# Two heads with rows in another order on the partitions, three stores in fifteen parts

## The chip, the cores and the metric

One core of a Trainium2 chip runs the program. The metric is device time in microseconds (us) of one execution. TensorE (PE), VectorE (DVE), ScalarE (ACT), GpSimd (POOL) and SyncE (SP) each run their own list of instructions in order; they wait for each other and for transfers on semaphores. Transfers (DMAs) are issued here by SP, ACT and POOL, and 16 DMA engines carry them out.

## The reference, cut to what matters

A decoder block for one token and all its gradients: attention with 32 heads over a cache of 8192 keys and values, and a gated MLP beside it. The outputs are the block's output and the gradients of its inputs, the caches among them.

```python
xn = _layernorm(x)
q  = (xn @ wq).reshape(1, 1, 32, 128).transpose(0, 2, 1, 3)
p  = softmax(einsum("bhqd,bhkd->bhqk", q, k_cache) * 128 ** -0.5)
o  = einsum("bhqk,bhkd->bhqd", p, v_cache)
out = x + o.transpose(0, 2, 1, 3).reshape(1, 1, 4096) @ wo + (silu(xn @ w1) * (xn @ w3)) @ w2
# returned: out, and the vjp of grad_out: d x, d k_cache, d v_cache, d wq, d wo, d w1, d w3, d w2
```

Each head reads 2 MB of K and 2 MB of V (bf16) and writes 2 MB of dK and 2 MB of dV, which are outer products: a row of dV is a probability times the head's output gradient, a row of dK a score gradient times q. No sum over the keys depends on their order.

## The kernel before

A head's K, V, dK and dV are tiles of 128 partitions with 64 rows of 128 elements each: partition p holds rows 64p to 64p + 63 of the head, 16 KB in one piece of device memory (`kc`, `vc`, `dkc`, `dvc`). The work runs over the heads in one loop, written out by hand; the program keeps the order in which each engine's instructions are written. While head h is finished, head h + 1 has its scores computed:

- `product` (L365, L367): DVE multiplies K or V with the broadcast vector into T, PE sums it over the elements.
- `row_max`, `exps`, `probs`, `row_dots`, `dscores`: softmax and its gradient, as [128, 64] tiles.
- `outer` (L380, L387, L394): the tile `ot` of dV, then that of dK. ACT makes 16 of its 64 columns, DVE the others, in two halves. After the second half POOL issues one store of 2 MB (L394). The last two heads are stored in halves by SP instead (L392).
- `load_v(h + 2)` and `load_k(h + 3)`, both on SP (L117, L110), each behind an `outer`.

Buffers set what may be in flight: three tiles for K, two for V, four for `ot` (`kpool`, `vpool`, `opool`). A load waits until the tile it overwrites has been read, an `outer` until the store of the `ot` four before it has landed.

Weights go beside that. `wq` is kept for eight heads at once (`wq_all`, 5 columns `ci` of 1024 elements on each partition) and overwritten with its gradient. When a group of eight heads is finished, `finish_steps` stores the gradient: the first column at once (L331), the other four go into the list `columns`. `outer_v` takes up to two from the list behind each following store of `ot` (L396), all on POOL. This falls behind the stores of dV and dK of head 9 for the first eight heads and of head 17 for the second; later groups are stored otherwise (`late`). SP also loads later columns of `wq` in `wq_columns` (L139), and ACT loads and stores `wo`.

Of the kernel before, what the change touches and what calls it, by code (L numbers as in the profile page):

```python
# [16 lines left out]
P = 128  # L17
# [4 lines left out]
def kernel(  # L22
# [22 lines left out]
    nc = tc.nc  # L45
    H = A_k_cache.shape[1]
# [5 lines left out]
    NC = D // P  # L52
    J = SK // P
    JH = J // 2
# [4 lines left out]
    GW = 8  # L59
# [19 lines left out]
    ps_o = ctx.enter_context(tc.tile_pool(name="ps_o", bufs=1, space=PSUM))  # L79
    ps_w = ctx.enter_context(tc.tile_pool(name="ps_w", bufs=3, space=PSUM))  # L80

    kc = A_k_cache.rearrange("b h (p j) d -> (b h) p j d", p=P)
    vc = A_v_cache.rearrange("b h (p j) d -> (b h) p j d", p=P)
    dkc = out_2.rearrange("b h (p j) d -> (b h) p j d", p=P)
    dvc = out_3.rearrange("b h (p j) d -> (b h) p j d", p=P)

    wq_v = A_wq.rearrange("(p ci) n -> p ci n", ci=NC)
    dwq_v = out_4.rearrange("(p ci) n -> p ci n", ci=NC)
# [9 lines left out]
    with tc.manual_schedule(engines=ORDERED):  # L98
# [8 lines left out]
        def load_k(h):  # L107
            pool, tag = ((opool, "o"), (vpool, "V"))[h] if h < 2 else (kpool, "K")
            Kt = pool.tile([P, J, DH], BF16, name="Kt", tag=tag)
            nc.sync.dma_start(Kt[:], kc[h])  # L110
            kv_tiles[h] = kv_tiles.get(h, [None, None])
            kv_tiles[h][0] = Kt

        def load_v(h):
            pool, tag = (opool, "o") if h == 1 else (vpool, "V")
            Vt = pool.tile([P, J, DH], BF16, name="Vt", tag=tag)
            nc.sync.dma_start(Vt[:], vc[h])  # L117
            kv_tiles[h] = kv_tiles.get(h, [None, None])
            kv_tiles[h][1] = Vt

# [3 lines left out]
        def store(dst, src, later=False):  # L124
            if later:
                late.append((dst, src))
            else:
                nc.gpsimd.dma_start(dst, src)
# [176 lines left out]
        def finish_steps(g):  # L305
            G_ = grp[g]
            wo_g = G_["wo"]
            on, on_bf = on_cols(g)
            behind_o.append((g, on_bf))
            yield  # L310
            assert not behind_o
            for r in range(GH):
                nc.scalar.activation(wo_g[:, r, :], g_bc_bf[:], ACTF.Copy, scale=on[:, r:r + 1])
                if r == 1:
                    yield
            if g == NG - 2:
                store(dwo_v[g], wo_g[:], True)
            else:
                nc.scalar.dma_start(dwo_v[g], wo_g[:])
            yield  # L320
            b, k = divmod(g, HB)
            for ci in range(NC):
                nc.scalar.activation(G_["wq"][:, ci, :], G_["dqbc"][:].rearrange("p h d -> p (h d)"),
                                     ACTF.Copy, scale=xn_col[:, ci:ci + 1])
            if g < NG - HB and k == HB - 1:
                cols = slice(b * GW * DH, (b + 1) * GW * DH)
                if g == NG - HB - 1:
                    store(dwq_v[:, :, cols], G_["wq_all"][:], True)
                else:
                    columns.extend((dwq_v[:, ci, cols], G_["wq_all"][:, ci, :]) for ci in range(NC))  # L330
                    nc.gpsimd.dma_start(*columns.pop(0))  # L331
            if g >= NG - HB:
                store(dwq_v[:, :, g * GH * DH:(g + 1) * GH * DH], G_["wq"], True)
            grp.pop(g)
# [35 lines left out]
        def outer(st, vec, w2, wf, dst, h, half):  # L370
            outer_v(st, vec, w2, dst, h, half, outer_s(st, vec, wf, half))

        def outer_s(st, vec, wf, half):
            if half == 0:
                st.ot = opool.tile([P, J, DH // 2, 2], BF16, name="ot", tag="o")
            j1 = (half + 1) * JH
            if wf is None:
                return j1
            for j in range(ACT_J):
                nc.scalar.activation(st.ot[:, j1 - ACT_J + j].rearrange("p a b -> p (a b)"), vec, ACTF.Copy,  # L380
                                     scale=wf[:, half, j:j + 1])
            return j1 - ACT_J

        def outer_v(st, vec, w2, dst, h, half, j1):
            j0 = half * JH
            n = j1 - j0
            nc.vector.tensor_tensor(st.ot[:, j0:j1],  # L387
                                    vec.rearrange("p (a b) -> p a b", b=2).unsqueeze(1).to_broadcast([P, n, DH // 2, 2]),
                                    w2[:, j0:j1, :].unsqueeze(2).to_broadcast([P, n, DH // 2, 2]), ALU.mult)
            rows = st.ot[:].rearrange("p j a b -> p j (a b)")  # L390
            if h >= H - TAIL:
                nc.sync.dma_start(dst[h][:, j0:j0 + JH, :], rows[:, j0:j0 + JH, :])  # L392
            elif half:
                nc.gpsimd.dma_start(dst[h], rows)  # L394
                for _ in range(2 if len(columns) > 2 else len(columns)):
                    nc.gpsimd.dma_start(*columns.pop(0))  # L396

        columns = []

        def row_max(st):  # L400
# [193 lines left out]
        for b in range(NB):  # L594
            rows, src = (P, w2t[:, b, :]) if b < NF else (REST, w2r)
# [37 lines left out]
        def gap():  # L633
            if steps and next(steps[0], "end") == "end":
                steps.pop(0)
# [13 lines left out]
        def wq_columns(h, part):  # L649
            b, r = divmod(h, GW)  # L650
            if 0 < b < H // GW - 1 and (r, part) in WQ_AT:
                load_wq(b + 1, *WQ_AT[r, part])

        for h in range(H - 1):
            n = new_head(h + 1) if h + 1 < H else None
            c = hs.pop(h)
            g, hh = divmod(h, GH)
            if n:
                product(n, "S", 0)
            probs(c)  # L660
            outer(c, c.do, c.P2, c.Pf, dvc, h, 0)
            if prev:
                keep_dq(prev)
            gap()
            row_dots(c)
            attend(c)
            turn_wq(c)
            if n:
                product(n, "S", 1)
            outer(c, c.do, c.P2, c.Pf, dvc, h, 1)  # L670
            if h + 2 < H:
                load_v(h + 2)
            wq_columns(h, 0)
            if hh == 1 and 0 < g < NG - 1:
                load_wo(g + 1, nc.scalar)
            gap()
            dscores(c)
            outer(c, c.q, c.U2, c.Uf, dkc, h, 0)
            keep_wq(c)
            if n:  # L680
                row_max(n)
                product(n, "DP", 0)
            outer(c, c.q, c.U2, c.Uf, dkc, h, 1)
            if h == 0:
                load_k(4)
            elif 1 < h < H - 3:
                load_k(h + 3)
            wq_columns(h, 1)
            wq_columns(h, 2)
            if h == H - 3:  # L690
                for dst, src in late:
                    store(dst, src)
            gap()
            if n:
                exps(n)
                product(n, "DP", 1)
            weights(c)
            gap()
            if hh == 1 and g + 1 < NG:
                steps.append(prep_steps(g + 1))  # L700
            if hh == 2:
                gap()
            prev = c

        c = hs.pop(H - 1)
# [1 line left out]
        probs(c)  # L707
        attend(c)
        turn_wq(c)
        outer(c, c.do, c.P2, None, dvc, H - 1, 0)  # L710
        row_dots(c)
        outer(c, c.do, c.P2, c.Pf, dvc, H - 1, 1)
        keep_dq(prev)
        while steps:
            gap()
        keep_wq(c)
        dscores(c)
        outer(c, c.q, c.U2, None, dkc, H - 1, 0)
        weights(c)
        keep_dq(c)  # L720
        on, on_bf = on_cols(g)
        on_sums(g, on_bf)
        outer(c, c.q, c.U2, None, dkc, H - 1, 1)
        dwq_t = tpool.tile([P, NC, GH * DH], BF16, name="dwq_t", tag="T")
        for ci in range(NC):
            nc.scalar.activation(dwq_t[:, ci, :], c.G["dqbc"][:].rearrange("p h d -> p (h d)"),
# [63 lines left out]
```

## Time and profile before

| | |
|---|---|
| time, median of 3 runs | 732.8 us (732.59 to 733.54) |
| time of the profiled execution | 732.82 us |
| its span, first to last instruction | 731.0 us |
| DVE, PE, ACT, POOL busy | 630.7, 558.0, 461.8, 47.4 us |
| bytes moved | 303.70 MB, 415 GB/s over the span |
| queue 1 (SP), queue 0 (POOL), queue 10 (ACT) | 155.41, 139.42, 7.87 MB |

The profile gives busy time for each engine, a row of 40 equal slices of the span for the DMA engines (busy tenths and GB/s), the chain of work that ended last (followed back from the end, each piece to what released it), groups of instructions, waits, and for every kind of DMA the median time from its issue to its landing. The trace behind it also records when each of a DMA's semaphore counts arrived, and start, duration, size and queue of every DMA packet, though not which of the 16 engines carried it.

### The profile page before, as it was taken

The page shows a single profiled execution, that of the slowest core. Times are in us where ns is not written, and L with a number is a line of the kernel's source. Part 1 is how long each engine was busy: PE and PEld are TensorE (multiplying, and loading weights), DVE is VectorE, ACT ScalarE, POOL GpSimd, SP SyncE. Part 2 cuts the span into 40 slices and gives each one's busy share as a digit, 9 for nine tenths or more (in the row PEclk, how much of TensorE's full clock was granted, in tenths as well). Part 3 has the DMA queues.
Part 4 walks back from the last instruction along what each step waited for, and adds up shares of the span by engine and source line. Part 5 has one row for each costly group of instructions (what it writes and reads, how often), then busy time and mean ns, then how long its engine had stood idle before and what let it go on. Part 6 is the DMA issues. An engine that isn't in the chain of part 4 may idle for free.

```text
span 731.0 us, 15785 instructions
## 1 busy us (share of the span) xinstructions
PE 558.0 (76%) x6513; PEld 325.8 (45%) x6513; DVE 630.7 (86%) x720; ACT 461.8 (63%) x1391; POOL 47.4 (6%) x92
## 2 busy tenths in 40 slices
PE   5776888887887797886788787578767888877860
PEld 3654445453544454443444444344444445444440
DVE  4789999999999796997899888689598998999990
ACT  2176666876768476775577756476476866777650
POOL 0010000000000100100000110100000000000100
PEclk9699788787888778778787677677888768877665
DMA  8999999999999999999999999999999999999992
GB/s 357 413 421 427 428 429 429 428 427 429 429 429 428 428 428 427 426 429 427 429 428 429 427 430 426 429 429 423 418 408 400 423 424 428 430 432 429 418 414 110
DMA packets 26790, 303.70 MB, mean 415 GB/s; under 512 B 3084, under 2 KB 3150, under 8 KB 9054
## 3 DMA queue, kind: packets, MB, share of 16 engines
q1 hardware_dynamic: 13778, 155.41, 50.6%
q0 software_dynamic: 11200, 139.42, 45.0%
q10 hardware_dynamic: 1740, 7.87, 2.6%
q8 instruction: 51, 0.84, 0.4%
q14 instruction: 21, 0.17, 0.1%
HBM read 151.34 MB, written 151.34 MB: 414 GB/s over the span
## 4 chain that ended last, share of the span: by engine, by line
DMA 53%; DVE 28%; PE 9%; ACT 5%; issue 2%; SPq 0%; ACTq 0%; DVEq 0%; POOLq 0%
DMA out_dram<-ot 44%; DVE T L365 13%; DVE ot L387 10%; DMA out_dram<-wo_g 4%; ACT ot L380 4%; DMA Vt<-in_A_v_cache_dram 3%; PE psS L367 2%; PE psDP L367 2%; DMA dbc<-in_B_w_dram 2%; DVE S_sb L402 1%; PE ob L429 1%; PE dx_ps L546 1%; PE up_ps L521 1%; DVE DP_sb L436 1%; PE gate_ps L521 1%
## 5 line engine op out<-in xcount | busy, mean ns | idle before, releaser
L367 PE MATMUL psDP<-T,ident_bf 128*128 128x512 bf16 x512 | 183.6, 523 | 59.9 <-DVE T L365 59.8
L367 PEld LDWEIGHTS <-ident_bf 128*128 128x128 bf16 x1024 | 121.6, 121 | 225.2 <-issue 174.5
L380 ACT ACTIVATE ot<-qs_g,Uf 128x128 bf16<-128x128 bf16 x496 | 151.5, 389 | 74.2 <-DMA out_dram<-ot 32.3
L380 ACT ACTIVATE ot<-do_g,Pf 128x128 bf16<-128x128 bf16 x504 | 154.0, 389 | 6.4 <-DMA out_dram<-ot 5.4
L367 PE MATMUL psS<-T,ident_bf 128*128 128x512 bf16 x512 | 149.8, 446 | 9.3 <-DVE T L365 9.2
L365 DVE TENSOR_TENSOR T<-Kt,qs_g 128x4096 bf16<-128x4096 bf16 x64 | 146.5, 2288 | 8.2 <-DMA Kt<-in_A_k_cache_dram 8.1
L365 DVE TENSOR_TENSOR T<-Vt,do_g 128x4096 bf16<-128x4096 bf16 x64 | 146.0, 2282 | 4.5 <-ACT do_g L284 2.5
L387 DVE TENSOR_TENSOR ot<-qs_g,U 128x3072 bf16<-128x3072 bf16 (+1 forms) x64 | 113.2, 1769 | 36.2 <-DMA out_dram<-ot 36.2
L387 DVE TENSOR_TENSOR ot<-do_g,P 128x3072 bf16<-128x3072 bf16 (+1 forms) x64 | 112.8, 1763 | 7.9 <-DMA out_dram<-ot 6.9
L394 POOL DMA_DIRECT2D out_dram<-ot x60 | 32.0, 534 | 573.7 <-DVE Uf L449 292.6
L451 PEld LDWEIGHTS <-Kt 128*128 128x128 bf16 x2048 | 58.1, 98 | 11.9 <-issue 9.8
L451 PE MATMUL ob<-U,Kt 128*128 128x1 bf16 x2048 | 57.3, 164 | 1.6 <-DVE U L444 1.5
L429 PEld LDWEIGHTS <-Vt 128*128 128x128 bf16 x2048 | 56.6, 97 | 0.0
L429 PE MATMUL ob<-P,Vt 128*128 128x1 bf16 x2048 | 56.0, 163 | 0.0
L406 PE MATMUL sm<-ident_f,mrow 128*128 128x128 f32 x64 | 19.2, 390 | 33.5 <-DVE mrow L404 33.5
L470 ACT ACTIVATE dq_diag<-ident_bf,odq 128x128 bf16<-128x128 bf16 x32 | 12.8, 400 | 45.8 <-DVE odq L466 45.8
L423 ACT ACTIVATE Pf<-E,rZ 128x16 f32<-128x16 f32 x32 | 9.8, 305 | 40.8 <-DVE rZ L419 40.7
L258 ACT COPY woT<-ps_t 128x512 bf16<-128x512 bf16 x40 | 23.0, 577 | 15.3 <-PE ps_t L253 15.3
L406 PEld LDWEIGHTS sm<-ident_f,mrow 128*128 128x128 f32 x64 | 12.0, 234 | 35.5 <-DVE mrow L404 33.8
L440 PE MATMUL sm<-rdot,ones_fc 128*128 128x1 f32 x64 | 11.3, 245 | 20.8 <-DVE junk L439 20.8
L440 PEld LDWEIGHTS sm<-rdot,ones_fc 128*128 128x128 f32 x64 | 10.6, 192 | 33.5 <-DVE junk L439 31.1
L402 DVE TENSOR_REDUCE S_sb<-psS 128x64 f32<-128x512 f32 x32 | 21.9, 684 | 3.2 <-PE psS L367 3.1
(160 smaller groups left out, 510.4 us busy)
## 6 DMA issues: line engine op xcount, KB each, us to landing
out_dram<-ot POOLq DMA_DIRECT2D x60, 2048.0 KB, 31.2
Kt<-in_A_k_cache_dram SPq DMA_DIRECT2D x32, 2048.0 KB, 25.9
Vt<-in_A_v_cache_dram SPq DMA_DIRECT2D x32, 2048.0 KB, 19.2
out_dram<-ot SPq DMA_DIRECT2D x8, 1024.0 KB, 16.4
out_dram<-wo_g ACTq DMA_DIRECT2D x6, 640.0 KB, 15.5
wo_g<-in_A_wo_dram ACTq DMA_DIRECT2D x6, 640.0 KB, 15.6
wq<-in_A_wq_dram SPq DMA_DIRECT2D x2, 1280.0 KB, 20.6
out_dram<-wq POOLq DMA_DIRECT2D x10, 256.0 KB, 39.8
```

Of the source, the lines that this page charges most:

```text
L258: nc.scalar.copy(woT[:], ps_t[:])
L365: nc.vector.tensor_tensor(T[:], src[:, :, ds_], vec[:, ds_].unsqueeze(1).to_broadcast([P, J, DHH]), ALU.mult)
L367: nc.tensor.matmul(ps[:], lhsT=ident_bf[:], rhs=T[:, :, RUN * i:RUN * (i + 1)], start=(half == 0 and i == 0), stop=(half == 1 and i == DHH ...
L380: nc.scalar.activation(st.ot[:, j1 - ACT_J + j].rearrange("p a b -> p (a b)"), vec, ACTF.Copy, scale=wf[:, half, j:j + 1])
L387: nc.vector.tensor_tensor(st.ot[:, j0:j1], vec.rearrange("p (a b) -> p a b", b=2).unsqueeze(1).to_broadcast([P, n, DH // 2, 2]), w2[:, j0: ...
L394: nc.gpsimd.dma_start(dst[h], rows)
L402: nc.vector.tensor_reduce(st.S[:], st.ps["S"][:], AX.X, ALU.add)
L406: nc.tensor.matmul(st.sm[:, 8:8 + P], lhsT=mrow[:].to_broadcast([P, P]), rhs=ident_f[:], start=True, stop=True, skip_group_check=True)
L429: nc.tensor.matmul(st.ob[:, 0:1], lhsT=st.V[:, j, :], rhs=st.P2[:, j, 0:1], start=(j == 0), stop=(j == J - 1), skip_group_check=True)
L440: nc.tensor.matmul(st.sm[:, 4:5], lhsT=ones_f, rhs=rdot[:], start=True, stop=True, skip_group_check=True)
L451: nc.tensor.matmul(st.ob[:, 1:2], lhsT=st.K[:, j, :], rhs=st.U2[:, j, 0:1], start=(j == 0), stop=(j == J - 1), skip_group_check=True)
L521: nc.tensor.matmul(ps[0:rows, b:b + 1], lhsT=block(wt[:, ci, :], b), rhs=xn_col_bf[:, ci:ci + 1], start=(ci == 0), stop=(ci == NC - 1))
```

## The change

For heads 9 and 17, K, V, dK and dV are placed on the partitions in another order (`rows_of` with `mixed`). A head's 128 pieces of 16 KB are numbered 0 to 127; before, partition p holds piece p. Now there are 16 lanes of 8 partitions: partition 8a + n holds piece 16n + a. Loads and stores of these heads use the same order, so each piece returns to its place.

Three of their tiles (dK of head 9, dV and dK of head 17) are no longer stored by one DMA of 128 partitions. POOL stores lanes 0 to 14, 120 partitions, and SP stores lane 15, 8 partitions, later (`behind_k`, behind `load_k` in the same head). Around each of the three, two columns of the `wq` gradient that were stored by two DMAs of 128 partitions are stored by three DMAs that each take both columns: 5 partitions ahead of the store, 78 and 45 behind it. The other tile of the two heads, dV of head 9, is still one DMA, followed by two single columns.

```diff
+    LANES = 16
+    MIXED = {9: "K", 17: "VK"}
+    def rows_of(ap, mixed):
+        if not mixed:
+            return ap.rearrange("b h (p j) d -> (b h) p j d", p=P)
+        return ap.rearrange("b h (n a j) d -> (b h) a n j d", a=LANES, j=J)
+    SPAN = P // LANES
...
-            nc.sync.dma_start(Kt[:], kc[h])
+            nc.sync.dma_start(Kt[:], rows_of(A_k_cache, h in MIXED)[h])
...
-            nc.sync.dma_start(Vt[:], vc[h])
+            nc.sync.dma_start(Vt[:], rows_of(A_v_cache, h in MIXED)[h])
...
-                    columns.extend((dwq_v[:, ci, cols], G_["wq_all"][:, ci, :]) for ci in range(NC))
-                    nc.gpsimd.dma_start(*columns.pop(0))
+                    wq_g = G_["wq_all"]
+                    def pair(ci):
+                        return lambda p0, p1: nc.gpsimd.dma_start(dwq_v[p0:p1, ci:ci + 2, cols], wq_g[p0:p1, ci:ci + 2, :])
+                    nc.gpsimd.dma_start(dwq_v[:, 0, cols], wq_g[:, 0, :])
+                    for ci, which in ((1, "V"), (3, "K")):
+                        if which in MIXED[b * GW + GW + 1]:
+                            columns.append(pair(ci))
+                        else:
+                            columns.extend((dwq_v[:, c, cols], wq_g[:, c, :]) for c in (ci, ci + 1))
...
+            out = rows_of({"K": out_2, "V": out_3}[dst], h in MIXED)[h]
             if h >= H - TAIL:
-                nc.sync.dma_start(dst[h][:, j0:j0 + JH, :], rows[:, j0:j0 + JH, :])
+                nc.sync.dma_start(out[:, j0:j0 + JH, :], rows[:, j0:j0 + JH, :])
             elif half:
-                nc.gpsimd.dma_start(dst[h], rows)
-                for _ in range(2 if len(columns) > 2 else len(columns)):
+                n = min(2, len(columns))
+                if dst in MIXED.get(h, ""):
+                    store_past(out, rows, columns.pop(0))
+                    n = 0
+                else:
+                    nc.gpsimd.dma_start(out, rows)
+                for _ in range(n):
                     nc.gpsimd.dma_start(*columns.pop(0))
+        def store_past(out, rows, pairs):
+            n = (LANES - 1) * SPAN
+            pairs(0, 5)
+            nc.gpsimd.dma_start(out[0:LANES - 1], rows[0:n])
+            pairs(5, 83)
+            pairs(83, P)
+            behind_k.append((out[LANES - 1], rows[n:P]))
...
             elif 1 < h < H - 3:
                 load_k(h + 3)
+            while behind_k:
+                nc.sync.dma_start(*behind_k.pop(0))
```

The calls of `outer` pass "K" or "V" in place of `dkc` and `dvc`.

More of the change, by code (lines that the diff above doesn't have):

```diff
@@ L80 @@
     ps_w = ctx.enter_context(tc.tile_pool(name="ps_w", bufs=3, space=PSUM))
[L82 to L85, printed above, removed]
+    LANES = 16
[5 more added lines that the diff above has]
+    SPAN = P // LANES
     wq_v = A_wq.rearrange("(p ci) n -> p ci n", ci=NC)
@@ L390, in outer_v @@
             rows = st.ot[:].rearrange("p j a b -> p j (a b)")
+            out = rows_of({"K": out_2, "V": out_3}[dst], h in MIXED)[h]
             if h >= H - TAIL:
-                nc.sync.dma_start(dst[h][:, j0:j0 + JH, :], rows[:, j0:j0 + JH, :])
+                nc.sync.dma_start(out[:, j0:j0 + JH, :], rows[:, j0:j0 + JH, :])
             elif half:
-                nc.gpsimd.dma_start(dst[h], rows)
-                for _ in range(2 if len(columns) > 2 else len(columns)):
-                    nc.gpsimd.dma_start(*columns.pop(0))
+                n = min(2, len(columns))
[5 more added lines that the diff above has]
+                for _ in range(n):
+                    nc.gpsimd.dma_start(*columns.pop(0))
+        def store_past(out, rows, pairs):
[5 more added lines that the diff above has]
+            behind_k.append((out[LANES - 1], rows[n:P]))
+        behind_k = []
         columns = []
@@ L660 @@
             probs(c)
-            outer(c, c.do, c.P2, c.Pf, dvc, h, 0)
+            outer(c, c.do, c.P2, c.Pf, "V", h, 0)
             if prev:
@@ L669 @@
                 product(n, "S", 1)
-            outer(c, c.do, c.P2, c.Pf, dvc, h, 1)
+            outer(c, c.do, c.P2, c.Pf, "V", h, 1)
             if h + 2 < H:
@@ L677 @@
             dscores(c)
-            outer(c, c.q, c.U2, c.Uf, dkc, h, 0)
+            outer(c, c.q, c.U2, c.Uf, "K", h, 0)
             keep_wq(c)
@@ L682 @@
                 product(n, "DP", 0)
-            outer(c, c.q, c.U2, c.Uf, dkc, h, 1)
+            outer(c, c.q, c.U2, c.Uf, "K", h, 1)
             if h == 0:
@@ L709 @@
         turn_wq(c)
-        outer(c, c.do, c.P2, None, dvc, H - 1, 0)
+        outer(c, c.do, c.P2, None, "V", H - 1, 0)
         row_dots(c)
-        outer(c, c.do, c.P2, c.Pf, dvc, H - 1, 1)
+        outer(c, c.do, c.P2, c.Pf, "V", H - 1, 1)
         keep_dq(prev)
@@ L717 @@
         dscores(c)
-        outer(c, c.q, c.U2, None, dkc, H - 1, 0)
+        outer(c, c.q, c.U2, None, "K", H - 1, 0)
         weights(c)
@@ L722 @@
         on_sums(g, on_bf)
-        outer(c, c.q, c.U2, None, dkc, H - 1, 1)
+        outer(c, c.q, c.U2, None, "K", H - 1, 1)
         dwq_t = tpool.tile([P, NC, GH * DH], BF16, name="dwq_t", tag="T")
```

## The prediction

> **What bounds the kernel now.** I read the page first: slices of the span, queues, chain.
>
> ```profile
> DMA  8999999999999999999999999999999999999992
> GB/s 357 413 421 427 428 429 429 428 427 429 429 429 428 428 428 427 426 429 427 429 428 429 427 430 426 429 429 423 418 408 400 423 424 428 430 432 429 418 414 110
> ...
> DMA 53%; DVE 28%; PE 9%; ACT 5%; issue 2%; SPq 0%; ACTq 0%; DVEq 0%; POOLq 0%
> DMA out_dram<-ot 44%; DVE T L365 13%; DVE ot L387 10%; DMA out_dram<-wo_g 4%; ACT ot L380 4%; DMA Vt<-in_A_v_cache_dram 3%; PE psS L367 2%; PE psDP L367 2%; DMA dbc<-in_B_w_dram 2%; DVE S_sb L402 1%; PE ob L429 1%; PE dx_ps L546 1%; PE up_ps L521 1%; DVE DP_sb L436 1%; PE gate_ps L521 1%
> ...
> out_dram<-ot POOLq DMA_DIRECT2D x60, 2048.0 KB, 31.2
> Kt<-in_A_k_cache_dram SPq DMA_DIRECT2D x32, 2048.0 KB, 25.9
> Vt<-in_A_v_cache_dram SPq DMA_DIRECT2D x32, 2048.0 KB, 19.2
> ```
>
> The 16 DMA engines are the bound: 428 GB/s in nearly every slice, and the chain waits 44% of the span for stores of `ot`. So only bytes, idle engines or an uneven share can change the time; the change moves no byte less. Two places are below 428: slices 28 to 33 and the end. Next, therefore, the DMA view of the last 31 us (a slice of its GB/s row is 0.775 us), and the same view of an early and a late stretch.
>
> ```profile
> GB/s 455 396 423 312 439 386 428 391 449 402 402 428 423 412 428 381 419 385 414 360 366 343 117 48 21 26 26 26 26 32 21 32 21 26 32 24 26 13 0 0
> ```
> ```profile
> out_dram<-ot POOLq DMA_DIRECT2D x9, 2048.0 KB, 18.0
> Vt<-in_A_v_cache_dram SPq DMA_DIRECT2D x5, 2048.0 KB, 15.0
> ```
> ```profile
> out_dram<-ot POOLq DMA_DIRECT2D x10, 2048.0 KB, 32.4
> Vt<-in_A_v_cache_dram SPq DMA_DIRECT2D x5, 2048.0 KB, 17.3
> ```
>
> From 718.6 to 729 us the rate is 26 GB/s, a sixteenth of 428: one engine works alone. The second and third fences are 60:150 and 560:660: a store of 2 MB took 18.0 us to land, later 32.4, while loads stayed at 15 to 17. The trace's semaphore record tells why. Every transfer of `ot` counts 16 arrivals, one an engine. For the store issued at 144.2 the 15th came at 161.8 and the 16th at 163.0; at 326.4: 358.3 and 363.0; at 638.4: 655.9 and 671.5. One engine falls behind, by 1, 5, then 15 us, where it stays because the other fifteen wait for the buffers that it still holds. The chain shows that hold:
>
> ```profile
> 599.04 32.33 DMA out_dram<-ot
> ...
> 638.42 33.10 DMA out_dram<-ot
> 671.54 1.76 DVE ot L387
> ...
> 713.41 0.19 DVEq L785
> ```
>
> In the packet record each packet starts 3 to 4 ns before its predecessor on the engine ends, so packets can be strung together. Undisturbed engines take 611 ns for 16 KB (26.9 GB/s). Stretches of the late one have none of the 51 instruction fetches and yet run slower: 154.95 to 202.11 us at 26.05 GB/s, which is 629 ns a packet. Strung back from the end, its last packet ends at 729.26; the others end between 716.9 and 718.5.
>
> **The change, part by part.** Sums are made on the profiled execution: last packet 729.26, span 731.0 (1.8 after it), time 732.82 (1.8 more), which is the median 732.8 to 0.02.
>
> (1) *The store without one lane.* 7680 packets for 60 stores are 128 a store, 8 an engine. Storing 15 lanes of 8 partitions takes 8 packets from one engine, three times: 24 packets. If that is the late engine, 24 x 0.629 = 15.1 us leave it. If it is another, the late one keeps all.
>
> (2) *The left lanes*, issued by SP: 8 partitions of 16 KB, three times. If they go to eight engines, one packet each, those get 3 x 0.61 = 1.8 us more, 1.9 on the late one if it is among them.
>
> (3) *The pairs.* The same 512 KB of `wq_all` in parts of 20, 312 and 180 KB in place of two DMAs of 256 KB. An even dealing of whole partitions needs a divisor: 5, 13 (of 78) and 15 (of 45) engines, my assumption. Then an engine gets between 16 and 40 KB where it had 32: at most 8 KB more, three times, 0.9 us; at least 1.8 less.
>
> (4) *Issue.* One more POOL DMA a tile, 0.54 us, the store itself 0.54 later, behind the part of five. POOL is 6% busy and its stores are behind 18 to 32 us of landing, so nothing. But POOL also waits for semaphores that are still in use:
>
> ```profile
> 426.27 0.54 POOL L396 DMA_DIRECT2D out_dram<-wq  x1 [3.04 <-DMA out_dram<-ot]
> 431.69 0.33 SPq L117 DMA_DIRECT2D Vt<-in_A_v_cache_dram  x1
> 436.63 0.33 SPq L110 DMA_DIRECT2D Kt<-in_A_k_cache_dram  x1
> 437.30 0.54 POOL L394 DMA_DIRECT2D out_dram<-ot  x1 [10.49 <-DMA out_dram<-ot]
> ```
> POOL's DMAs go round eight semaphores, and each waits until the eighth before it has landed. Two more in head 17 make the store of K17 (422.16) wait for that of V16 (landed 426.0) and that of K18 (443.78) for V17's (450.3; its 15th arrival 444.3): 1 to 6.5 us later, behind a ring filled for 20 us. Taken as 0, with 6.5 as the upper end.
>
> (5) *SP.* The left lanes stand behind `load_k` and wait for the finished `ot`: in head 9 from 244.08 to 249.64, in head 17 from 415.71 to 422.16. Behind them stands only `load_v`, at 263.92 and 431.69, so 9 us or more hide it. V17's lane is issued some 10 us after its store and lands in some 15, inside the store's own 38. Zero; uncovered, some 6 us once.
>
> (6) *Rows in another order.* Loads and stores of heads 9 and 17 remain packets of 16 KB. No row shows this order. Bounds: 0, or doubled packets (rival C). I take 0: the nearest row, 64 rows of 1280 B on half the partitions, took 55 ns a packet, in line with 84 ns for 2048 B. Less than 0 is excluded, as 611 ns is the fastest seen.
>
> (7) *Which engine.* The last DMA of ACT has five rows of 256 B, and one of these packets (717.235) is in the late engine's string. Their five closing packets came at 715.713, 715.788, 715.863, then 716.554 and 718.038, the last on the late engine. Dealt in order, 75 ns apart, the late one is fourth or fifth. If POOL deals parts in rotation from the first engine, five parts take the first five, the 15 parts run from the sixth round to the fourth, and the fifth is left out. 5 + 13 + 15 + 15 = 48 then ends where it began. I find both numberings plausible, neither shown; hence the miss below.
>
> Sum for the late engine: 15.1 - 1.9 - 0.9 = 12.3 us less, 729.3 - 12.3 = 717.0. The others end at 718.5, get up to 1.8 + 0.5 more, and win back what they idled for it: slices 28 to 33 lack 78 GB/s against 429, 78/429 x 18.3 = 3.3 us. 718.5 + 2.3 - 3.3 = 717.5, which ends last. Can the computing follow? The wait up to 671.54 could end at 655.9; next the DVE needs V31, which landed at 685.2 and was first used at 692.9, so its chain can move 7.7 us earlier; 3.3 are needed. Last packet 717.5, so 717.5 + 1.8 + 1.8 = **721.1 us**. Ends: perfect sharing, mean end of the others 717.4 + 10.8/16 - 3.3 = 714.8, and slices 38 and 39 filled too (26 GB/s short, 1.1 us), 713.7, time 717.3; no idle won back, 720.8, time 724.4.
>
> What the skill says of part 7: the Trainium skill, DMA: Bandwidth & Descriptors, section "Latency and other measured facts", has engines 7 and 15 usually slower. By that the skip would miss, which part 7's packets speak against. The dealing assumed in parts 3 and 7 (the largest count up to 16 that divides, in rotation on POOL's queue, the lowest engines on ACT's) is stated in its section "Why a DMA increments its semaphore by 16 and not by 1"; no run here shows it.
>
> The Trainium skill, SBUF — State Buffer, section "Door 1: The DMA port swizzle", puts partitions 32 apart on the same port. By it lanes of eight neighbouring partitions could meet at a port, which speaks for rival C; the 55 ns row does not show it.
>
> **Rivals.**
>
> B: *the skip misses.* The late engine keeps its 15.1 us and gets parts 2 and 3: between 1.9 - 1.8 = 0.1 and 1.9 + 0.4 = 2.3 us more, 732.9 to 735.1. For it: no row shows POOL's dealing, or that engine numbers of two queues agree. Against it: part 7's fifth place in both counts. 0.13, of which 0.05 for a late engine in eighth or last place (735.1 or 733.3).
>
> C, the slower side: *two engines meet in the new order.* Place: the eight transfers of heads 9 and 17, 64 packets an engine. Price: 64 times what a packet gains over 611 ns; at 800 ns it eats the 12 us, and doubled it costs 39, so 732.8 - 12 + 39 = 760. For it: nothing in the rows; against it the 55 ns, and that half the traffic goes elsewhere at any time. 0.07, decided from 800 ns on.
>
> D: *hit, but some is lost* to POOL's semaphore waits (up to 6.5 us) or packets between 611 and 800 ns: 724.4 to 731. 0.09.
>
> **How the numbers follow.** A hit as summed: 0.71, 717.3 to 724.4, at 721.1. With D that is 0.80 in 717.3 to 731, the range; B and C are left out. A difference of 0.2%, 1.5 us, is what a measurement of this kernel can tell. Faster: 0.71 + 0.09 = 0.80. Same: of B the part below 734.3, 0.07. Slower: the rest of B 0.06 and C 0.07, 0.13.
>
> **What would show it.** Right: the lone 26 GB/s at the end is gone or under 2 us; the 16th arrival of late stores is within 5 us of the 15th; stores at 560:660 land in under 25 us; slices 28 to 33 are at 425 or more; the chain's wait for `ot` is under 30%. Part 1 alone is right if the lag drops by 4 to 5 us after K9 (250) and by 8 to 10 after head 17 (420). Wrong: a lone engine still at work for 10 us at the end (B); packets of heads 9 and 17 over 700 ns, GB/s under 400 near 200 to 290 or 375 to 460 us (C); POOL waits over 10 us after 426 (D). I would also be wrong if computing ended last: then the rate falls off for all engines at once, before the last store is issued.

## The result, and the profile after

The changed kernel takes 743.13 us (median of 4 runs, 741.55 to 745.22); the kernel before, beside it on the same chip, 732.69 us (732.34 to 733.54). The ratio is 1.0142, 95% interval [1.0116, 1.0169]: 10.4 us slower, where 721.1 was predicted. The profiled execution took 741.55 us with a span of 739.1. The ratios below leave out one run as slow, 740.64 us of the run without SP's 8 partitions, because it lies over 1.5% above the fastest of its kernel.

The page of the kernel after: slices (of 18.5 us here), chain, DMA issues.

```profile
DMA  9999999999999999999999999999999999999995
GB/s 356 412 422 426 430 427 427 430 430 423 410 394 427 427 427 401 428 421 429 420 364 412 427 410 398 368 413 423 427 390 395 433 419 430 430 428 430 424 419 233
...
DMA 51%; DVE 31%; PE 9%; ACT 5%; issue 1%; SPq 0%; ACTq 0%; DVEq 0%; POOLq 0%
...
out_dram<-ot POOLq DMA_DIRECT2D x57, 2048.0 KB, 31.2
Kt<-in_A_k_cache_dram SPq DMA_DIRECT2D x32, 2048.0 KB, 23.8
Vt<-in_A_v_cache_dram SPq DMA_DIRECT2D x32, 2048.0 KB, 18.9
...
out_dram<-ot POOLq DMA_DIRECT2D x3, 1920.0 KB, 38.5
```

The three stores of 120 partitions are there, and the bytes are the same (303.70 MB). But the GB/s row, flat at 426 to 430 before from slice 4 to 27, has holes: slice 12 (394), 21 (364), 25 and 26 (398 and 368). The windows view, by 100 us, shows what kind of hole this is. Its last three columns are granted clock, busy share of the DMA engines, GB/s; first the kernel before, then after.

```profile
200.00:300.00 100.00, 78.46 (x876) 43.80 (x873) 86.65 (x94) 65.22 (x199) 9.14 (x17) 0.78 1.01 428
300.00:400.00 100.00, 77.69 (x944) 44.93 (x944) 88.16 (x97) 69.87 (x215) 4.82 (x9) 0.77 1.01 428
400.00:500.00 100.00, 73.51 (x801) 42.02 (x800) 82.29 (x92) 63.50 (x192) 8.64 (x16) 0.73 1.01 427
```
```profile
200.00:300.00 100.00, 79.82 (x931) 45.50 (x930) 86.08 (x94) 67.94 (x209) 10.12 (x18) 0.74 1.01 413
300.00:400.00 100.00, 76.73 (x952) 45.10 (x950) 83.51 (x91) 63.75 (x197) 4.81 (x9) 0.80 1.01 410
400.00:500.00 100.00, 66.57 (x767) 38.84 (x766) 76.13 (x82) 58.74 (x181) 9.87 (x17) 0.71 1.01 404
```

The engines are no less busy (1.01), they move less: 15, 18 and 23 GB/s short for 100 us each is 56 x 100 / 427 = 13 us. So the packets got longer. The packet record says where. All packets' durations together, over 16 engines, are 720.91 us before and 734.37 after, 13.5 more. Of these 12.7 are packets of 16 KB, of loads and stores, lasting longer than the undisturbed 611 ns (5.1 us an engine above that before, 17.8 after). Most of it, 10.6 of the 17.8, lies in three places: 200 to 222 us (loads of K9 and V9), 362 to 400 (loads of K17 and V17), 440 to 480 (stores behind the split ones of head 17).

The end, in the DMA view from 700 to 740 us (1 us a column), and from 560 to 660:

```profile
GB/s 430 436 417 387 410 429 416 442 422 439 409 429 419 425 396 445 408 401 410 427 441 410 438 409 401 410 372 402 296 275 211 151 111 84 49 52 41 5 0 0
```
```profile
out_dram<-ot POOLq DMA_DIRECT2D x10, 2048.0 KB, 31.8
Vt<-in_A_v_cache_dram SPq DMA_DIRECT2D x5, 2048.0 KB, 16.0
```

The 10 us at 26 GB/s of a single engine are gone. In their place is a staircase from 727 to 737 us: engines end one after the other. Each engine's end can be read from the 16 arrivals of the last small DMA of SP (`dx_bf`): before, the mean engine ends at 718.8 and the last 11.0 us behind it; after, the mean ends at 731.8 and the last 6.1 behind it. So 4.8 us were won by evening, while the mean end moved back by 12.9, about what the longer packets add (12.7); 8.1 us is the difference of the spans.

### The profile page after: what moved, and what is told of

It is laid out like the page before. It is cut to its first block, busy times and chain, and to the rows that moved or that the text cites. A ratio compares the mean times of both kernels' runs of the same rounds, so it can differ in the third digit from the quotient of the medians.

```text
span 739.1 us, 15799 instructions
## 1 busy us (share of the span) xinstructions
PE 560.7 (76%) x6513; PEld 328.9 (45%) x6513; DVE 630.6 (85%) x720; ACT 461.7 (62%) x1391; POOL 50.1 (7%) x95
## 2 busy tenths in 40 slices
DMA packets 26982, 303.70 MB, mean 411 GB/s; under 512 B 3276, under 2 KB 3342, under 8 KB 9246
## 4 chain that ended last, share of the span: by engine, by line
DMA 51%; DVE 31%; PE 9%; ACT 5%; issue 1%; SPq 0%; ACTq 0%; DVEq 0%; POOLq 0%
DMA out_dram<-ot 44%; DVE T L380 14%; DVE ot L402 11%; DMA Kt<-in_A_k_cache_dram 4%; ACT ot L395 3%; PE psS L382 2%; DMA out_dram<-wo_g 2%; PE psDP L382 2%; DMA dbc<-in_B_w_dram 2%; DVE S_sb L432 1%; PE ob L459 1%; PE dx_ps L576 1%; DVE DP_sb L466 1%; PE up_ps L551 1%; PE gate_ps L551 1%
## 5 line engine op out<-in xcount | busy, mean ns | idle before, releaser
L395 ACT ACTIVATE ot<-do_g,Pf 128x128 bf16<-128x128 bf16 x504 | 154.0, 389 | 13.0 <-DMA out_dram<-ot 10.6
L436 PE MATMUL sm<-ident_f,mrow 128*128 128x128 f32 x64 | 20.8, 419 | 44.0 <-DVE mrow L434 44.0
```

Of the source, the lines that this page charges most:

```text
L436: nc.tensor.matmul(st.sm[:, 8:8 + P], lhsT=mrow[:].to_broadcast([P, P]), rhs=ident_f[:], start=True, stop=True, skip_group_check=True)
```

## The experiments

All are compared with the kernel before on the same chip. "Longer packets" is what the 16 KB packets of loads and stores took above 611 ns each, summed and divided by 16 engines; the kernel before has 5.1 us. It comes from one profiled execution of each kernel.

| run | what it is | median, us | ratio, interval | longer packets |
|---|---|---|---|---|
| after | the change: 16 lanes, parts of 5, 78, 45 | 743.13 | 1.0142 [1.0116, 1.0169] | 17.8 |
| e1_order | order alone | 745.34 | 1.0127 [1.0073, 1.0180] | 16.5 |
| e3_loads | order in loads alone | 738.79 | 1.0069 [1.0054, 1.0084] | 10.8 |
| e4_stores | order in stores alone | 739.24 | 1.0071 [1.0049, 1.0093] | 10.7 |
| e8_lanes64 | order alone, 64 lanes of 2 | 733.22 | 0.9997 [0.9988, 1.0006] | 5.6 |
| e11_lanes32 | order alone, 32 lanes of 4 | 733.50 | 0.9997 [0.9987, 1.0006] | 5.4 |
| e14_lanes8 | order alone, 8 lanes of 16 | 775.75 | 1.0579 [1.0556, 1.0602] | 34.7 |
| e2_split | split alone, old order | 738.11 | 1.0052 [1.0024, 1.0080] | 10.6 |
| e6_six | the change, parts of 6, 52, 70 | 747.78 | 1.0175 [1.0139, 1.0211] | 17.3 |
| e9_full64 | the change with 64 lanes | 732.63 | 1.0005 [0.9977, 1.0033] | 8.6 |
| e10_six64 | the same, parts of 6, 52, 70 | 736.95 | 1.0046 [1.0029, 1.0063] | 9.9 |
| e13_nopairs | e9 with whole pairs | 738.75 | 1.0066 [1.0038, 1.0093] | 10.4 |
| e12_notail | e9 without SP's 8 partitions | 730.08 | 0.9942 [0.9925, 0.9960] | 7.6 |
| e5_pairs | parts alone, whole stores | 734.54 | 1.0015 [1.0006, 1.0025] | 6.7 |
| e7_columns | skip by the columns of `wq` | 732.05 | 0.9981 [0.9972, 0.9991] | 7.9 |

### The two halves of the change, each alone

The order is kept and the split taken out:

```diff
+    ORDER_IN = ORDER_OUT = (9, 17)
+    SPLIT = {}
...
-                if dst in MIXED.get(h, ""):
+                if dst in SPLIT.get(h, ""):
```

> The new order of rows in loads and stores of heads 9 and 17, every store in one DMA of 128 partitions, the columns stored as before. Theory 1 (the order itself costs: packets of these transfers get in each other's way; in the changed kernel 16 KB packets took 204 engine-us more than before, 12.7 us on each of 16 engines): 740 to 753 us, slower than the changed kernel if the skip gave it something, with packets over 1 us near 200 to 230, 280 and 360 to 480 us, and the late engine's 16th arrivals again 10 us or more behind. Theory 2 (the loss comes from the divided stores, their pairs and POOL's semaphore waits; the order is free): 732 to 735 us, packets as before.

The split is kept on the old order (`ORDER_IN = ORDER_OUT = ()`, `SPLIT = MIXED`, and the three stores take their rows in the old order):

> The same three stores of 120 partitions between parts of 5, 78 and 45, the last 8 partitions by SP, but all rows in the old order. Theory 1: no packets over 1 us in heads 9 and 17; 718 to 724 us if the left-out engine is the late one, 732.5 to 735 if the dealing of a plain store of 120 partitions leaves out another. Theory 2: 738 us or more, with POOL waiting for transfers 10 us or more after head 17.

The order alone costs 1.27% (9 us by the ratio, 11 by the medians), nearly the whole loss against the kernel before. The split alone is no gain either: 0.5% slower. That is the time of its second theory, but POOL's waits, which this theory blamed, cost 1.1 us where they are tried by themselves (below). In its arrivals the late engine is still the 16th, 15.1 us behind the median (store of 636.2 us; 16.9 before, store of 638.4); it is only 8.7 us behind the 15th, because others have become late. So a plain store of 120 neighbouring partitions did not leave the late engine out, while the pattern of lanes does (below).

### Loads or stores

`ORDER_IN` and `ORDER_OUT` are set one at a time, without the split. In either, rows of dK and dV of the two heads come out in another order than the reference has.

> The new order in the four loads of K and V of heads 9 and 17 alone; stores and columns as before, so dK and dV of these two heads come out in another order of rows. Theory 1, from the changed kernel's packets (about 98 of the 204 engine-us lie in 200 to 220 and 360 to 400 us, where these loads run): 6 us more than before, 738 to 742 us. Theory 2: 732 to 734 us.

> The new order in the four stores of dK and dV of heads 9 and 17 alone; loads and columns as before, so dK and dV of these two heads come out in another order of rows. Theory 1, from the changed kernel's packets (about 80 to 90 of the 204 engine-us near 280 and 440 to 480 us): 5 to 6 us more than before, 737 to 742 us; if it was the 15 parts that met there, and not the order of the store, 732 to 734. Theory 2: 732 to 734 us.

0.69% and 0.71%: both sides pay, and together 1.40% they make up, within the intervals, the 1.27% of both. For the loads the place is plain. The DMA view from 196 to 226 us (0.75 us a column), with the order in loads alone, and then with 64 lanes:

```profile
GB/s 459 481 371 393 371 328 306 240 328 328 306 350 350 393 437 393 502 371 393 415 502 415 393 350 350 328 328 371 393 415 502 393 393 415 459 459 371 437 459 371
```
```profile
GB/s 437 393 393 459 437 437 415 437 437 393 459 415 481 393 437 393 502 371 437 393 437 437 437 437 437 437 415 459 393 459 415 459 371 481 371 459 415 459 415 415
```

The dip to 240 to 330 GB/s lies where K9 and V9 are loaded. From 200 to 222 us the packets of loads take 708 ns on the mean there (612 before), and those of the stores beside them, of other heads in the old order, 663 (614 before). The stores in the new order show it elsewhere: packets of up to 2.4 us between 440 and 480 us.

### How far apart the engines work

Only `LANES` changes from the run with the order alone, to 64:

> As the kernel with the new order alone, but with 64 lanes of 2 pieces in place of 16 lanes of 8: partition 2a + n holds piece 64n + a. An engine that takes eight neighbouring partitions then reads four pieces in a row and jumps once, where it jumped 256 KB after every piece; on the SBUF side nothing differs from the new order. If the packets meet on the SBUF side: 741 to 748 us, 16 KB packets of 1.1 us near 200 to 220 and 360 to 400 us as there. If they meet in device memory, because of the jumps: 733 to 738, packets under 0.8 us.

to 32:

> The new order alone in loads and stores of heads 9 and 17, as in the run with 16 lanes of 8 (745.3) and in that with 64 lanes of 2 (733.2), here 32 lanes of 4, which puts neighbouring engines 32 KB apart in device memory instead of 16 or 64. If the loss shrinks with that distance (theory), the time lies between: 735 to 742, with packets of heads 9 and 17 of some 700 ns on the mean. If the loss is a matter of how many partitions of one lane follow each other in SBUF, it is half of that of 16 lanes too; then the two cannot be told apart by this run. If only the exact 16 KB is bad, 733 to 734.

and to 8:

> The new order alone in loads and stores of heads 9 and 17, with 8 lanes of 16 partitions: partition 16a + n holds piece 8n + a. Neighbouring lanes are 16 KB apart as with 16 lanes, but each engine jumps 128 KB from piece to piece, not 256. If lanes 16 KB apart make the packets long (theory), the loads' packets at 200 to 222 and at 362 to 400 us are at some 680 ns on the mean, as with 16 lanes (614 before), and the time is 740 or more. If the jump of 256 KB does it (rival), they stay at 612 to 616, as with 32 and 64 lanes (jumps of 512 KB and 1 MB), and the time is 733 to 734. If the eight lanes go to eight engines only, these fall behind and the time says nothing; the packets still tell.

(The first of these texts says that an engine reads four pieces in a row. With 64 lanes partition 2a + n holds piece 64n + a, so it too jumps after each piece, by 1 MB.) With 64 and with 32 lanes the cost is gone, and with 32 it is not halved, as its theory had it; the packets of loads from 200 to 222 us are back at 612 ns. With 8 lanes they are at 857 ns, worse than the 703 of the order alone with 16. Part of the 42 us lost there is something else, since the eight lanes also leave engines idle. The four loads of these heads then count 8 arrivals as their packets land, where the other loads of K and V count 16, and the windows view has the busy share at 0.94 and 0.95 in the stretches of heads 9 and 17:

```profile
200.00:300.00 100.00, 68.67 (x759) 39.13 (x761) 70.81 (x77) 54.94 (x169) 7.23 (x13) 0.68 0.94 341
...
400.00:500.00 100.00, 67.19 (x772) 38.42 (x773) 73.32 (x80) 56.76 (x174) 7.03 (x13) 0.74 0.95 351
```

So it is not the jump of exactly 256 KB (with 8 lanes it is 128 KB, and slower), and not the order as such. What decides is the number of lanes: 8 and 16 are slow, 32 and 64 free. Two readings of that are left. If an engine takes eight neighbouring partitions, neighbouring engines stand 16 KB apart in device memory with 16 lanes, 32 with 32 and 64 with 64; but the record does not say which engine carries which packet. And the jump from piece to piece inside a lane grows with the lanes too (128 and 256 KB slow, 512 KB and 1 MB free). No run here separates closeness from jump.

The SBUF side is written the same in all four orders: 128 partitions of 16 KB, in order. So the difference comes in with the addresses in device memory, unless the number of lanes also changes which partitions an engine takes. The rule of ports that spoke for rival C (the Trainium skill, SBUF — State Buffer, section "Door 1: The DMA port swizzle") goes by the partition alone, so by itself it does not tell 16 lanes from 32. The cost that rival C feared was real all the same.

### Which engine is left out

The change with parts of 6, 52 and 70, so that another engine is left out:

```diff
-            pairs(0, 5)
+            pairs(0, 6)
...
-            pairs(5, 83)
-            pairs(83, P)
+            pairs(6, 58)
+            pairs(58, P)
```

> The whole change, but the parts are 6, 52 and 70 partitions (6, 13 and 14 engines if dealt evenly) in place of 5, 78 and 45, so that the 15 parts leave out the sixth engine and not the fifth. If the change's skip does hit the slow engine (the one whose 16 KB packets are nearly all over 612 ns) and is worth something: its 16th arrivals are 14 us or more behind the others again, and the time is 746 to 752 us, slower than the changed kernel's 743. If the skip is worth nothing there: 742 to 745, as the changed kernel.

Then the change with 64 lanes (60 by POOL, 4 by SP), with both sets of parts:

```diff
-    LANES = 16
+    LANES = 64
...
-            n = (LANES - 1) * SPAN
+            k = LANES - LANES // 16
+            n = k * SPAN
...
-            nc.gpsimd.dma_start(out[0:LANES - 1], rows[0:n])
+            nc.gpsimd.dma_start(out[0:k], rows[0:n])
...
-            behind_k.append((out[LANES - 1], rows[n:P]))
+            behind_k.append((out[k:LANES], rows[n:P]))
```

> The whole change, but with 64 lanes of 2 partitions: store of 60 lanes (120 partitions) with the parts of 5, 78 and 45, the last 4 lanes by SP. If the new order lost its time because neighbouring engines work 16 KB apart in device memory (theory), the packets of heads 9 and 17 stay near 611 ns, as with 64 lanes alone (733.2 against 733.8), the skip keeps the 3 to 4 us that it is worth between the kernel of the change and the one with parts of 6, 52 and 70, and the pairs cost their 1: 729 to 732 us. If the sum of the prediction was right but for the order, 721. If the loss comes from the split itself, beside the order (rival; the split on the old order had 738.1), 736 to 739.

> As the run with 64 lanes and the whole change, but parts of 6, 52 and 70, so that the 120 partitions leave out the next engine instead of the fifth. Theory (the fifth is the slow one): the slow engine is last again at the stores, and the time is 3 to 5 us over the run with parts of 5, 78 and 45. Rival (it does not matter which is left out): the two agree within 1.5 us.

With 64 lanes the change loses its 10 us (1.0142 to 1.0005) and lands just above the 729 to 732 that was expected; it still gains nothing over the kernel before. (With 64 lanes alone the kernel before took 733.2 beside it, not the 733.8 of the text.)

The late engine is known in the packet record by its string: 70% or more of its packets last over 612 ns, with a mean near 630. Its packets end with the 16th arrival before, with parts of 6 in both orders, and with whole pairs. With parts of 5 they end in the middle of the 16: at 1.6 us after the first arrival of the store of 643.0 us in the kernel after, at 2.7 to 2.9 us with 64 lanes. So for the stores by lanes the fifth place was right, and it is worth 0.33% between the kernel after and its twin with parts of 6, 0.41% with 64 lanes: 2.4 and 3.0 us by the ratios (4.2 and 4.3 by the medians). For each pair the intervals overlap, so the size is rough.

But the 16th is then another engine, whose packets last 611 ns: for the store at 643.0 the arrivals behind the first are 0.1, 0.2, 0.3, 0.9, 1.2, 1.6, 1.6, 2.4, 2.4, 3.8, 6.0, 9.0, 9.4, 12.5 and 16.6 us. Five engines have become late that were not. With 64 lanes it is 13.7 us from first to last, and the rate falls off in a staircase too (700 to 740 us):

```profile
GB/s 433 411 411 419 416 439 422 431 422 408 426 390 418 415 417 408 387 311 293 289 276 230 131 69 55 41 10 0 0 0 0 0 0 0 0 0 0 0 0 0
```

The 12 runs of the change with 64 lanes lie between 730.07 and 740.23, six below the fastest of the kernel before (732.48) and four above its slowest (735.32). On the mean nothing is won.

### What the split itself costs

The parts around whole stores in the old order (5, 39 and 84):

> Only the parts: two columns at a time in parts of 5, 39 and 84 partitions around the three stores, which are whole and in the old order (one POOL DMA more a tile, as in the change). If POOL's semaphores and small parts are free, as predicted: 733 to 735 us. If they cost what the divided stores in the old order lost (3.8 us): 736 to 739, with POOL waiting 10 us or more for transfers behind head 17.

```profile
427.57 0.59 POOL L422 DMA_DIRECT2D out_dram<-ot  x1 [10.36 <-DMA out_dram<-ot]
438.36 0.62 POOL L339 DMA_DIRECT2D out_dram<-wq  x1 [10.20 <-DMA out_dram<-ot]
...
453.03 0.57 POOL L415 DMA_DIRECT2D out_dram<-ot  x1 [9.34 <-DMA out_dram<-ot]
```

These rows of the timeline (start, duration, engine, line, in brackets the idle time before and what ended it) show that the two more DMAs make POOL wait for its semaphores and put the stores off, K17 from 422.16 to 427.57 and K18 from 443.78 to 453.03; and still it costs 0.15%, 1.1 us, in all (0.4 to 1.8 by the interval).

Then the change with 64 lanes without SP's three DMAs (8 partitions of each of the three tiles are not stored), and with each pair as one DMA:

```diff
-            behind_k.append((out[k:LANES], rows[n:P]))
```

> The whole change with 64 lanes, but without the three DMAs of SP: the last 8 partitions of the three tiles (0.4 MB in all) are not stored, so the time is read with that. By bytes alone that is 24 packets of 303.7 MB, 0.9 us of 16 engines. If the longer packets after each split come from those 8 packets on eight engines (theory), the packets of 280 to 310 and of 440 to 500 us are back near 611 ns and the time is 727 to 730, without runs of 735 and more. If they come from the parts or from the store of 120 partitions itself (rival), they stay and the time is that of the run with the tails less 1: 730 to 732 with the same spread.

```diff
-            pairs(0, 5)
...
-            pairs(5, 83)
-            pairs(83, P)
+            pairs(0, P)
```

> The whole change with 64 lanes, but the pair of columns beside each of the three tiles is one DMA behind the store, not parts of 5, 78 and 45: the store of 120 partitions then leaves out another engine each time and not the slow one. If the parts are what lengthens the packets (theory), there are about 0.5 us an engine of longer packets and the time is 733 to 734, as with 64 lanes alone. If it is the store of 120 partitions with its tail (rival), the longer packets stay and the time is that of the run with parts of 6, 52 and 70: 736 to 738.

The longer packets stay in both: 7.6 us without the tail (8.6 with it, so the tail is 1 of the 3.5 over the kernel before), 10.4 without the parts. The parts around whole stores have 6.7, 1.6 over the kernel before. By elimination most of the longer packets come with the store of 120 partitions, but no run has that store without both tail and parts, so this is argued and not shown. They are mostly packets of stores, some of 1 to 2.9 us, 15 to 50 us after a split store is issued (280 to 310 and 440 to 500 us). The first expectation's 727 to 730 was just missed, a run of 740.64 remains, and the packets stay long, as its rival had it. The second run landed near where the rival put it (738.75 for 736 to 738).

### The skip without the split stores

The kernel before, with the old order and whole stores; the columns of `wq` of the first three groups carry the skip instead:

```diff
+                four = [part(0, 2, 0, 5), part(2, 5, 0, P - 8), part(0, 2, 5, 83), part(0, 2, 83, P)]
+                behind_k.append(part(2, 5, P - 8, P))
...
-                    columns.extend((dwq_v[:, ci, cols], G_["wq_all"][:, ci, :]) for ci in range(NC))
+                    columns.extend(four)
```

> The kernel before, with another carrier for the skip: all tiles of heads in the old order and whole; of the wq gradient of the first three groups of eight heads, columns 0 and 1 are stored in parts of 5, 78 and 45, columns 2 to 4 in 15 parts of 120 partitions behind the part of 5, and their last 8 partitions by SP. It takes 3 x 48 KB from the fifth engine, 5.5 us, less 0.9 for the pairs and 0.7 for SP's. If the skip hits the slow engine and the order was what cost: the 16th arrival of late stores falls from 15 to about 11 us behind, the time to 729 to 732 us. If the divided DMAs themselves cost: 734 to 738.

Here the engines stay together: from first to 16th arrival the stores of 633.8 and 641.4 us need 2.3 and 4.9 us, with the late engine among the others (about 11 us behind was expected), and the chain hardly waits for stores:

```profile
DMA 41%; DVE 31%; PE 20%; ACT 4%; issue 1%; SPq 0%; DVEq 0%; ACTq 0%
DMA Kt<-in_A_k_cache_dram 30%; DVE T L373 15%; DVE ot L395 9%; PE psS L375 7%; DMA out_dram<-ot 5%; PE ob L438 3%; ACT ot L388 3%; DMA Vt<-in_A_v_cache_dram 3%; PE psDP L375 2%; DMA out_dram<-wo_g 2%; PE ob L460 2%; DMA dbc<-in_B_w_dram 2%; DVE DP_sb L445 1%; DVE S_sb L411 1%; PE ps_q L263 1%
```

Stores are 5% of it, 44% before. Yet only 0.19% is won (1.1 us by the medians; all ten runs lie below the fastest of the kernel before). Of the 16 arrivals of `dx_bf` the last comes 3.6 us earlier (729.8 to 726.2) and the mean 4.1 us later (718.8 to 723.0). So about half of the evening is that the other engines became slower: all packets' durations together grew by 4.2 us an engine, 720.91 to 725.15, while the idle time of the engines between 690 us and the last packet fell by 8, from 176 to 47 engine-us.

The 3.6 us at the last packet (729.26 to 725.67) do not all reach the end either. POOL's closing instruction, a DRAIN that starts with its last store, ends 1.0 us behind the last packet before (730.28), and 3.6 us behind it here (729.31). The store of `dwq_t` ahead of it is issued 4.0 us later (712.37 to 716.37). SP's last wait is over at 726.6, so the end of this version follows POOL's DRAIN and no longer the last packet. It is the one version here that stores everything and is steadily faster than both kernels.

## Why the prediction was wrong, point by point

Two steps failed, each by some 10 us: step 6, which makes the change a loss, and the sum of the skip, without which there is no gain. Between 721.1 and 743.1 lie 22 us. The order alone costs 9.3, and where its cost is gone (64 lanes) the change takes 1.0005 of the kernel before, still 12 us above 721.1.

**Step 6, the new order, taken as 0, failed.** Its upper bound, rival C at 0.07, was the case that came. Its signs are there: 394 GB/s in the slice of 203 to 222 us, 364 at 370 to 388, 398 and 368 at 443 to 480; the loads' packets at 703 and 695 ns. The row chosen as nearest (64 rows of 1280 B, 55 ns a packet) shows small packets from half the partitions, and nothing of where in device memory the pieces lie that are moved at the same time; it was nearest in form and not in the thing that mattered. Rival C's price was mis-sized too. It was to begin at 800 ns, for only the 64 packets an engine in the new order, though its own sign said 700. By the 800 the 703 ns belong to rival D, whose time ended at 731. The packets beside them grew as well, and so a mean of 686 ns over all 16 KB packets of those stretches was enough for some 10 us.

**Steps 1 and 7, the skip, were right in kind.** The fifth place was hit, and the lone 26 GB/s at the end is gone. Part 1's own sign came true as well: by its string the late engine is 3.7 us behind the median of the 16 arrivals for the store of 232 us, 0.1 for that of 275, and 3 to 12 us ahead of it behind head 17 (449 to 465). That the fifth place was hit is no proof of the numbering, as only the fifth and the sixth were tried, and the store of plain rows with the same parts missed.

The dealing that was taken from the Trainium skill, DMA: Bandwidth & Descriptors, section "Why a DMA increments its semaphore by 16 and not by 1", fits what parts of 5 and of 6 did with stores by lanes, and not the store of plain rows. The Trainium skill's section "Latency and other measured facts" on the same page, by which the skip would have missed, does not fit if that dealing holds; no trace numbers the engines.

**The sum behind it failed.** It let 15.1 us leave the late engine and kept the others together, ending at 718.5 with "up to 1.8 + 0.5 more". In the kernel after they do not stay together: the last one, 6.1 us behind the mean, is no longer the late engine. Against parts of 6 the skip is worth 2.4 to 4.3 us, not the 12.3 of the sum, and the split that carries it costs 3.4 us when it misses (64 lanes, parts of 6: 0.46%), where rival B had 0.1 to 2.3. From runs of their own, order 9.3 + split 3.4 - skip 3.0 = 9.7 us, against the 10.4 measured; since the interval of the order alone is 5.4 to 13.2 us, the agreement is in part luck.

**Step 2** (1.8 to 1.9) was low rather than wrong: without SP's DMAs the ratio is 0.6% smaller (4.6 us, with intervals of 0.2 to 0.3% each way; 3.1 us by the medians, which keep the run of 740.64), of which 0.9 us are bytes. That each goes to eight engines is borne out: each counts 8 arrivals as its packets land. **Step 3** (0.9): 1.1 measured, with the waits of step 4 in it.

**Step 4, POOL's waits, taken as 0.** The mechanism was right and its upper end a little low:

```profile
419.44 0.60 POOL L422 DMA_DIRECT2D out_dram<-ot  x1 [6.71 <-issue]
...
434.25 0.58 POOL L422 DMA_DIRECT2D out_dram<-ot  x1 [10.33 <-DMA out_dram<-ot]
...
444.20 0.70 POOL L339 DMA_DIRECT2D out_dram<-wq  x1 [9.37 <-DMA out_dram<-ot]
...
458.53 0.57 POOL L415 DMA_DIRECT2D out_dram<-ot  x1 [9.13 <-DMA out_dram<-ot]
```

K17 is issued 12.1 us later than before and K18 14.7, and 7.1 of these were V17's delay already (412.3 before); 5.0 and 7.6 are left, where 1 to 6.5 was said. The wait of 10.33 us is also rival D's sign, but the kernel before has one of 10.49 (437.30). The run with the parts alone shows what such waits are worth with the small parts: 1.1 us. That the rest is hidden by a ring filled for some 20 us was argued, and no run shows it. **Step 5** held: the two lanes of head 17 are issued by SP from 422.10 to 429.93, the next load behind them at 439.67. They land 20.9 and 24.9 us after their issue, not in some 15.

Of the signs that were to show the prediction right, the lone engine and the gap of the 16th arrival behind the 15th (4.2 us) came true. The latter says little, since the 15th was late itself; 16th against median (14.6) would have been the sign to ask for. Stores at 560 to 660 us landed in 31.8 us, not under 25; the chain waits 44% for `ot`, not under 30%; slices 28 to 33 go down to 390 GB/s, where 425 or more was asked.

What stays open: why a store dealt to fifteen engines lengthens the packets of stores behind it (neither the tail nor the parts explain it, and the columns, dealt to fifteen as well, cost 2.8 us an engine of the same kind). Open as well is whether the closeness of the lanes or the jump inside them makes 8 and 16 lanes slow. An explanation by how far neighbouring engines are out of step would be near, but no run shows it.

## What to carry to other kernels

Where the DMA engines are the bound, read busy share and GB/s of a stretch side by side: with packets of the same size, full share with less GB/s means longer packets, which no count of packets foretells. An access pattern that is the same in bytes and packet size can still differ in which addresses of device memory are moved at the same time, and here that cost 1.27%; measure one transfer before the pattern is costed at nothing. Taking work from the one late engine gains only as much as the others stay together: ask for the mean and the spread of all sixteen ends, not for the last alone.

## What the runs showed of the hardware

- Four loads and four stores of 2 MB in pieces of 16 KB, in an order by lanes: a load packet from 200 to 222 us takes 703 ns with 16 lanes and 857 with 8, and 612 with 32 or 64 lanes, as in the plain order. Stores of other tiles beside the loads slow down too (614 to 663 ns, with the order in loads alone).
- Stores of 120 partitions by lanes, with five parts ahead of each, left out the engine they were aimed at (7th of 16 arrivals at 643.0 us); the same stores of plain neighbouring rows left it last.
- New waits of POOL of some 10 us on semaphores in use, together with the small parts, cost 1.1 us (0.4 to 1.8).
- In the version with the skip by the columns the last packet ended 3.6 us earlier and the program 1.0 us; POOL's closing DRAIN ended 3.6 us behind the last packet, 1.0 before.
